# Block-wise linear attention ahead of two MLP layers: states kept without zero halves and met by the queries in quarters of the array, outputs and state sums in the score banks

## The chip, the cores and the metric

One core of a Trainium2 chip runs the whole kernel. The metric is the device time of one execution in microseconds (us); lower is better. The engines are PE (TensorE matmul; PEld is its loading of the stationary operand), DVE (VectorE), ACT (ScalarE), POOL (GpSimd) and SP, which issues the transfers. Each engine runs its own queue strictly in order; an instruction that must wait holds everything behind it on its engine.

## The reference

Attention with a decay per head, then two MLP layers. The part that matters:

```python
for b in range(nb):                        # blocks of a sequence, one after the other
    intra = einsum('bhic,bhjc->bhij', qb, kb) * Dmask      # Dmask[i,j] = lam**(i-j), i >= j
    intra = einsum('bhij,bhjd->bhid', intra, vb)
    inter = einsum('bhid,bhde->bhie', qb * lam_pow, kv_state)
    out[:, :, sl] = intra + inter
    kv_state = lam_block * kv_state + einsum('bhsd,bhse->bhde', kb * rev_pow, vb)
x = out with heads side by side            # (1536, 512)
h = x @ w_in;  x = where(h > 0, h, exp(min(h, 0)) - 1) @ w_out            # layer 0
h = x @ w_in2; y = (max(h, 0) + alpha * min(h, 0)) @ w_out2               # layer 1
```

There are 2 sequences of 768 positions, 8 heads of 64 channels, a model width of 512 and a hidden width of 2048. The kernel takes blocks of 128 positions (the decay makes that the same sum), so it has 12 blocks, 6 for each sequence. Block 0 and block 6 start from an empty state.

## The kernel before

**Attention, one block n.** The 8 heads stand as 4 pairs `pr`, head = 2*pr + `hs`. `load(n)` brings keys and queries (channels on the partitions, the two heads of a pair on partitions 0 to 63 and 64 to 127) and values and keys (positions on the partitions), 512 KB each. `scores(n)` makes the transposed scores in two PSUM banks, one for each `hs`, four pairs side by side (L201). `mask(n)` multiplies each bank by the decay and leaves the result in SBUF as `sm` (DVE, L208, two instructions). `scale(n)` makes the decayed keys `kd_t` and the decayed queries `qs_t` on POOL. `state(n)` sums keys times values into a bank of its own, `stp` (L223). `outputs(n)` makes, in a third kind of bank `po`, values times masked scores (L256, eight matmuls with 64 output rows each) and adds state times queries (L262): here the state of a pair is a 128 x 128 tile whose two off-diagonal quarters are zero, so one full-array matmul serves two heads. Blocks 0 and 6 have no L262. `new_state(n)` scales the old state on ACT (L235, four instructions) and adds `stp` on DVE (L241); the last block of a sequence has none. `keep(n)` copies the outputs into the MLP's operand as a rounded part `xh` (ACT, L274) and the rest `xl` (DVE, L275).

**MLP.** 96 items i: for each layer, four groups of four hidden tiles, three token chunks of 512 and the four tiles of a group. `up(i)` is 12 matmuls of 128 x 512 (three products of rounded parts and rests, four channel groups each, L362); ACT, DVE and POOL turn the result into `gh_t` and `gl_t`. `down(i)` is 12 matmuls (L400) and comes two items later (LAG = 2). Chunk 0 of x is blocks 0 to 3, so `up(0)` needs those four.

**Weights.** They arrive as 64-bit numbers; `split_w` makes a rounded part and a rest in six steps: ACT L125, DVE L126, L128 and L131, ACT L134, POOL L135. Each step is put off by a number of ticks of the program's own count and goes into its engine's queue where that tick falls. `wi` (into the hidden width) and `wo` (out of it) come in pairs of hidden tiles, 1 MB each.

**Order.** It is written out by hand (manual schedule). Four blocks come first (AHEAD), then one block with each item 0 to 7, then items alone:

```python
n = AHEAD + i
p_ = block_a(n)        # state(n); scores(n + 1); mask(n + 1)
up(i)
weights(i)
block_b(n, p_)         # outputs(n); new_state(n); keep(n); load(n + 4); scale(n + 2)
for e in range(4):
    if i < LAG: tick()
    else:       down(i - LAG, e)
```

So scores and mask of a block stand one `up` ahead of the outputs that use them. Items 0 and 1 have no `down`.

Of the kernel before, what the change touches and what calls it, by code (L numbers as in the profile page):

```python
# [7 lines left out]
F32 = mybir.dt.float32  # L8
# [3 lines left out]
ALU = mybir.AluOpType  # L12

B, H, S, D = 2, 8, 768, 64
C = 128
NBLK = B * S // C
PB = S // C
# [16 lines left out]
def attention_two_layers(  # L34
# [30 lines left out]
    def bank(name):  # L65
        return ps.tile([128, 512], F32, tag="ps", name=name)
# [30 lines left out]
    def load_w(c):  # L97
        n, part = divmod(c, 2)
        l, k = divmod(n, NPAIR)
        wi, wo = wts[l]  # L100
        r = wraw.tile([128, 2048], U32, tag="raw", name="raw")
        if part == 0:
            nc.sync.dma_start(
                out=r.rearrange("p (c f) -> p c f", c=NCC),
                in_=wi[:, k * 512:(k + 1) * 512].rearrange("(c p) f -> p c f", p=128))
        else:
            nc.sync.dma_start(
                out=r.rearrange("p (f e) -> p f e", f=2),
                in_=wo[k * 256:(k + 1) * 256, :].rearrange("(f p) e -> p f e", p=128))
        raw[c] = r  # L110
# [30 lines left out]
    def new_x(t, nm):  # L141
# [9 lines left out]
    rev = dm.rearrange("p s a i -> p a s i")[:, :, :, C - 1:C]  # L151
    sms = [wsp.tile([128, 1024], F32, tag=tag, name="sm").rearrange(
        "p (s a i) -> p s a i", s=2, a=NP) for tag in ("wil", "woh")]
    st2 = wsp.tile([128, 1024], F32, tag="wol", name="st").rearrange(
        "p (s a i) -> p s a i", s=2, a=NP)
    st = [st2[:, 0], st2[:, 1]]

    ld = {}
# [47 lines left out]
    def mask(n):  # L206
        for hs, p_ in enumerate(sc.pop(n)):
            nc.vector.tensor_tensor(  # L208
                out=sms[n % 2][:, hs], in0=p_.rearrange("p (a i) -> p a i", a=NP),
                in1=dm[:, hs], op=ALU.mult)  # L210

    cur = [0]

    def state(n):
        if n not in kd:
            return None
        kd_ = kd.pop(n)
        v_ = vs[n][0]
        p_ = bank("stp")
        for pr in range(NP):  # L220
            for hs in range(2):
                h = 2 * pr + hs
                nc.tensor.matmul(  # L223
                    out=p_[hs * 64:(hs + 1) * 64, pr * D:(pr + 1) * D], lhsT=kd_[:, h, :],
                    rhs=v_[:, h, :], start=pr == 0, stop=True, skip_group_check=True)
        return p_[:, 0:NP * D].rearrange("p (a d) -> p a d", a=NP)

    def new_state(n, p_):
        if p_ is None:
            return  # L230
        first = n % PB == 0
        old, new = st[cur[0]], st[1 - cur[0]]
        if not first:
            for pr in range(NP):
                nc.scalar.mul(new[:, pr, :], old[:, pr, :], lamc[:, pr, :])  # L235
        for hs in range(2):
            a, b = hs * 64, (hs + 1) * 64
            if first:
                nc.vector.tensor_copy(new[a:b, :, a:b], p_[a:b])
            else:  # L240
                nc.vector.tensor_tensor(  # L241
                    out=new[a:b, :, a:b], in0=p_[a:b], in1=new[a:b, :, a:b],
                    op=ALU.add)
        cur[0] = 1 - cur[0]

    def outputs(n):
        v_, _ = vs.pop(n)
        po = bank("po")
        sm_ = sms[n % 2]
        s_ = st[cur[0]]  # L250

        inter = n % PB > 0
        for pr in range(NP):
            for hs in range(2):
                h = 2 * pr + hs
                nc.tensor.matmul(  # L256
                    out=po[hs * 64:(hs + 1) * 64, pr * C:(pr + 1) * C],
                    lhsT=v_[:, h, :], rhs=sm_[:, hs, pr, :], start=pr == 0,
                    stop=not inter, skip_group_check=True)
        if inter:  # L260
            for pr in range(NP):
                nc.tensor.matmul(  # L262
                    out=po[:, pr * C:(pr + 1) * C], lhsT=s_[:, pr, :], rhs=qs[n][:, pr, :],
                    start=False, stop=True, skip_group_check=True)
        qs.pop(n, None)
        return po

    def keep(n, po):
        t, o = divmod(n * C, CH)
        if o == 0:  # L270
            new_x(t, "x")
        pv = po.rearrange("p (a i) -> p a i", a=NP)
        xh_ = xh[t][:, :, o:o + C]
        nc.scalar.copy(xh_, pv)  # L274
        nc.vector.tensor_tensor(  # L275
            out=xl[t][:, :, o:o + C], in0=pv, in1=xh_.bitcast(F32), op=ALU.subtract)
# [6 lines left out]
    def block_a(n):  # L283
        p_ = state(n)
        if n + 1 < NBLK:
            scores(n + 1)
            mask(n + 1)
        return p_

    def block_b(n, p_):  # L290
        po = outputs(n)
        new_state(n, p_)
        keep(n, po)
        if n + 4 < NBLK:
            load(n + 4)
        if n + 2 < NBLK:
            scale(n + 2)

    def begin():
        nc.sync.dma_start(out=row[:, 128:128 + H], in_=lam.rearrange("h a -> a h"))  # L300
        load(0)
        load(1)
        load_w(0)
        load(2)
        load(3)
# [32 lines left out]
        for s_ in st:  # L338
            nc.gpsimd.memset(s_, 0.0)
        scores(0)  # L340
        scale(0)
        mask(0)
        scale(1)
        split_w(0, (5, 6, 7, 9, 11), 4)

# [108 lines left out]

    with tc.manual_schedule():
        begin()
        for n in range(AHEAD):
            weights(n - AHEAD)
            p_ = block_a(n)
            for _ in range(3):  # L460
                tick()
            block_b(n, p_)
            if n < 2:
                load_w(2 - n)
            if n == 3:
                load_w(3)
            for _ in range(3):
                tick()
        for i, _ in enumerate(items):
            if i == 2:  # L470
                nc.sync.dma_start(out=alpha_sb, in_=alpha)
            if i == 20:
                nc.vector.tensor_scalar(
                    out=beta, in0=alpha_sb, scalar1=-1.0, scalar2=1.0, op0=ALU.mult,
                    op1=ALU.add)
            n = AHEAD + i
            p_ = block_a(n) if n < NBLK else None
            up(i)
            weights(i)
            if n < NBLK:  # L480
                block_b(n, p_)
            for e in range(4):
                if i < LAG:
                    tick()
                else:
                    for c0, c1 in parts(i - LAG, e):
                        down(i - LAG, e, c0, c1)
        for i in range(len(items) - LAG, len(items)):
            for e in range(4):
                for c0, c1 in parts(i, e):  # L490
                    down(i, e, c0, c1)
# [50 lines left out]
```

## Time and profile before

| | us |
|---|---|
| three timed runs | 586.23, 587.03, 587.05 (median 587.03) |
| the profiled execution, its own time | 586.05 |
| its span, first to last instruction | 584.1 |
| PE busy in the span | 575.3 (98%) |
| DVE, ACT, POOL busy | 271.8, 240.9, 227.9 |

The profile is of one execution. Positions below are us from the start of its span. 1.95 us of its time lie around the span.

### The profile page before, as it was taken

The numbers are of one execution on the slowest core, as the hardware profiler recorded it, in microseconds if no ns is written. First come the engines' busy times: TensorE is split into PE (matmuls) and PEld (weight loads), VectorE is DVE, ScalarE is ACT, GpSimd is POOL, SyncE is SP. The second block draws the span as 40 slices with busy tenths as digits, with TensorE's granted clock in tenths as the row PEclk, the third lists the DMA queues.
The fourth block names the chain that finished last, engine by engine and source line by source line (L and its number), as shares of the span: only waits on it lengthen the run. The fifth ranks groups of instructions, "written<-read, shape, count | busy, mean of one in ns | idle before, by whom it ended". The sixth has DMA issues, their size and how long they took to land.

```text
span 584.1 us, 7319 instructions
## 1 busy us (share of the span) xinstructions
PE 575.3 (98%) x2960; PEld 475.6 (81%) x2960; DVE 271.8 (47%) x363; ACT 240.9 (41%) x374; POOL 227.9 (39%) x156
## 2 busy tenths in 40 slices
PE   7999999999999999999999999999999999999997
PEld 6886788888888888888888888888888888888886
DVE  7777444753534542543645731443553551641332
ACT  2536354565435444544654442533324323432220
POOL 3756512454324344344233444434415334432221
PEclk9999999999999999999999999999999999999999
DMA  8985300342202122122102212222204110000111
GB/s 323 412 329 172 101 1 6 140 143 73 73 0 85 60 73 72 73 72 73 53 20 81 68 69 73 72 74 72 73 0 141 31 46 0 2 0 1 72 73 72
DMA packets 18307, 49.23 MB, mean 84 GB/s; under 512 B 1250, under 2 KB 1506, under 8 KB 18274
## 3 DMA queue, kind: packets, MB, share of 16 engines
q1 hardware_dynamic: 18274, 48.77, 23.7%
q8 instruction: 23, 0.38, 0.3%
q14 instruction: 10, 0.08, 0.0%
HBM read 45.62 MB, written 3.15 MB: 83 GB/s over the span
## 4 chain that ended last, share of the span: by engine, by line
PE 93%; DVE 2%; DMA 2%; ACT 1%; POOL 0%; issue 0%; SPq 0%; DVEq 0%
PE dn L400 44%; PE up L362 43%; DMA raw<-in_w1i 2%; PE sc L201 1%; PE po L256 1%; PE po L262 1%; PE warm L281 1%; DVE wt L128 1%; PE stp L223 1%; ACT st L235 0%; DVE acc L416 0%; DVE wt L131 0%; POOL wol L135 0%; DVE st L241 0%; DVE wt L126 0%
## 5 line engine op out<-in xcount | busy, mean ns | idle before, releaser
L384 POOL TENSOR_TENSOR gl_t<-g_t,gh_t 128x512 fp32r<-128x512 f32 x96 | 125.1, 1304 | 320.4 <-ACT gh_t L383 265.9
L373 ACT ACTIVATE r_t<-up 128x512 f32<-128x512 f32 x96 | 57.3, 597 | 187.2 <-PE up L362 187.2
L383 ACT CAST gh_t<-g_t 128x512 fp32r<-128x512 f32 x96 | 59.6, 621 | 110.9 <-DVE g_t L377 57.9
L416 DVE TENSOR_TENSOR acc<-dn,acc 128x512 f32<-128x512 f32 (+1 forms) x73 | 46.9, 676 | 75.7 <-PE dn L400 75.7
L400 PE MATMUL dn<-gh_t,wol 128*128 128x512 f32 x192 | 74.9, 390 | 1.3 <-POOL wol L135 1.3
L381 DVE SCALAR_TENSOR_TENSOR g_t<-r_t,beta,up 128x512 f32<-128x512 f32 x48 | 35.7, 743 | 86.2 <-ACT r_t L373 77.5
L400 PE MATMUL dn<-woh,gl_t 128*128 128x512 f32 (+1 forms) x196 | 75.4, 385 | 0.0
L400 PE MATMUL dn<-woh,gh_t 128*128 128x512 f32 (+1 forms) x196 | 75.4, 385 | 0.0
L400 PE MATMUL dn<-wol,gh_t 128*128 128x512 f32 (+1 forms) x196 | 75.4, 385 | 0.0
L400 PE MATMUL dn<-gh_t,woh 128*128 128x512 f32 x192 | 75.3, 392 | 0.0
L400 PE MATMUL dn<-gl_t,woh 128*128 128x512 f32 x192 | 74.8, 389 | 0.0
L377 DVE SCALAR_TENSOR_TENSOR g_t<-r_t,up 128x512 f32<-128x512 f32 x48 | 32.8, 683 | 63.0 <-ACT r_t L376 63.0
L362 PE MATMUL up<-xh,wih 128*128 128x512 f32 x192 | 52.2, 394 | 0.0
L362 PE MATMUL up<-xl,wih 128*128 128x512 f32 x192 | 51.4, 389 | 0.0
L362 PE MATMUL up<-xh,wil 128*128 128x512 f32 x192 | 51.4, 389 | 0.0
L362 PE MATMUL up<-yh,wih 128*128 128x512 f32 x192 | 51.3, 389 | 0.0
L362 PE MATMUL up<-yl,wih 128*128 128x512 f32 x192 | 51.3, 389 | 0.0
L362 PE MATMUL up<-yh,wil 128*128 128x512 f32 x192 | 51.3, 389 | 0.0
L126 DVE TENSOR_SCALAR wt<-wt 128x1024 uint32<-128x1024 uint32 x32 | 29.7, 927 | 33.5 <-ACT wt L125 33.5
L400 PEld LDWEIGHTS dn<-gh_t,wol 128*128 128x128 f32 x192 | 36.0, 188 | 9.2 <-POOL wol L135 1.7
L400 PEld LDWEIGHTS dn<-woh,gl_t 128*128 128x128 f32 x196 | 36.8, 188 | 7.4
L400 PEld LDWEIGHTS dn<-wol,gh_t 128*128 128x128 f32 x196 | 36.8, 188 | 7.4
(57 smaller groups left out, 796.2 us busy)
## 6 DMA issues: line engine op xcount, KB each, us to landing
raw<-in_w1i SPq DMA_DIRECT2D x8, 1024.0 KB, 5.6
raw<-in_w1o SPq DMA_DIRECT2D x8, 1024.0 KB, 4.8
raw<-in_w2i SPq DMA_DIRECT2D x8, 1024.0 KB, 5.4
raw<-in_w2o SPq DMA_DIRECT2D x8, 1024.0 KB, 4.9
blk<-in_kqT SPq DMA_DIRECT2D x12, 512.0 KB, 6.9
blk<-in_vk SPq DMA_DIRECT2D x10, 512.0 KB, 8.2
out<-acc SPq DMA_DIRECT2D x11, 256.0 KB, 2.1
blk<-in_vk SPq DMA_DIRECT2D x2, 256.0 KB, 6.4
```

The source lines that it names most:

```text
L126: later(gaps[0], lambda: nc.vector.tensor_scalar(out=tu, in0=tu, scalar1=3, scalar2=None, op0=ALU.logical_shift_left))
L128: later(gaps[1], lambda: nc.vector.scalar_tensor_tensor(out=tu, in0=lower, scalar=29, in1=tu, op0=ALU.logical_shift_right, op1=ALU.bitwise ...
L201: nc.tensor.matmul(out=ps_[hs][:, pr * C:(pr + 1) * C], lhsT=z[a:b, 0, pr, :], rhs=z[a:b, 1, pr, :], start=True, stop=True)
L223: nc.tensor.matmul(out=p_[hs * 64:(hs + 1) * 64, pr * D:(pr + 1) * D], lhsT=kd_[:, h, :], rhs=v_[:, h, :], start=pr == 0, stop=True, skip_ ...
L362: nc.tensor.matmul(out=p_, lhsT=w[:, cc, fo:fo + 128], rhs=x[t][:, cc, :], start=n == 0, stop=n == 3 * NCC - 1)
L373: nc.scalar.activation(r, p_, AF.Relu, scale=-1.0)
L377: later(1, lambda: nc.vector.scalar_tensor_tensor(out=g, in0=r, scalar=-1.0, in1=p_, op0=ALU.add, op1=ALU.max))
L381: later(1, lambda: nc.vector.scalar_tensor_tensor(out=g, in0=r, scalar=beta[:, f:f + 1], in1=p_, op0=ALU.mult, op1=ALU.add))
L383: later(2, lambda: nc.scalar.copy(gh_, g))
L384: later(3, lambda: nc.gpsimd.tensor_tensor(out=gl_, in0=g, in1=gh_.bitcast(F32), op=ALU.subtract))
L400: nc.tensor.matmul(out=p_, lhsT=a, rhs=b, start=first and n == 0, stop=last and n == 2)
L416: nc.vector.tensor_tensor(out=a, in0=p_, in1=a, op=ALU.add)
```

## The change

States are kept as 64 x 64 blocks, one for each head: a pair's two heads lie on partitions 0 to 63 and 64 to 127 of the same 64 columns. State times queries becomes eight matmuls for each block, 64 rows by 64 columns of the array each, in the order (o, hs) = (0,0), (1,0), (0,1), (1,1), where `o` is the half of the output partitions (pair pr = 2*pp + o). Outputs are written into the two banks in which the block's scores were, state sums into the other half of the first of them; the banks `po` and `stp` go. The new state is made by four DVE instructions (scale and add in one), behind the last state-times-queries matmul into the first bank; the four ACT instructions of before go. `keep` works on each bank by itself: two ACT and two DVE instructions of 256 columns in place of one each of 512, and ACT's first one comes behind DVE's reading of the state sums in the same bank. Since x's channels now stand in another order on the partitions, layer 0's `wi` is loaded by four transfers of 64 partitions in place of one of 128. The block's work is written in another order.

```diff
-        if part == 0:
+        if part == 0 and l == 0:
+            for o in range(2):
+                for hs in range(2):
+                    nc.sync.dma_start(
+                        out=r.rearrange("p (s a f) -> p s a f", s=2, a=2)[
+                            o * 64:(o + 1) * 64, hs],
+                        in_=wi[:, k * 512:(k + 1) * 512].rearrange(
+                            "(a o s d) f -> o s d a f", a=2, o=2, s=2)[o, hs])
+        elif part == 0:
...
+    def outputs(n):
...
+        for pp in range(2):
+            for o, hs in QUAD:
+                pr = 2 * pp + o
                 nc.tensor.matmul(
+                    out=p_[hs][o * 64:(o + 1) * 64, pp * C:(pp + 1) * C],
+                    lhsT=v_[:, 2 * pr + hs, :], rhs=sm_[:, hs, pr, :], start=pp == 0,
+                    stop=n % PB == 0, skip_group_check=True)
+        kd_ = kd.pop(n, None)
+        if kd_ is not None:
+            for pr in range(NP):
+                for hs in range(2):
...
+                        out=p_[0][hs * 64:(hs + 1) * 64, c0:c0 + D], lhsT=kd_[:, h, :],
+                        rhs=v_[:, h, :], start=False, stop=True, skip_group_check=True)
+        if n % PB:
...
+                    nc.tensor.matmul(
+                        out=p_[hs][o * 64:(o + 1) * 64, pp * C:(pp + 1) * C],
+                        lhsT=s_[a:b, pr, :], rhs=qs[n][a:b, pr, :], start=False, stop=True,
...
     def new_state(n, p_):
-        if not first:
             for pr in range(NP):
-                nc.scalar.mul(new[:, pr, :], old[:, pr, :], lamc[:, pr, :])
...
+                nc.vector.scalar_tensor_tensor(
+                    out=new[:, pr, :], in0=old[:, pr, :], scalar=lamc[:, pr, :],
+                    in1=p_[:, pr, :], op0=ALU.mult, op1=ALU.add)
...
+    def block(n):
+        p_, more = outputs(n)
+        if more:
+            new_state(n, p_)
+        keep(n, p_)
...
+    def ahead(n):
+        if n < NBLK:
+            scores(n)
+            mask(n)
...
-        scores(0)
+        ahead(0)
         scale(0)
-        mask(0)
+        ahead(1)
         scale(1)
...
         for n in range(AHEAD):
             weights(n - AHEAD)
-            p_ = block_a(n)
+            block(n)
             for _ in range(3):
                 tick()
-            block_b(n, p_)
+            if n + 2 <= AHEAD:
+                ahead(n + 2)
...
-            p_ = block_a(n) if n < NBLK else None
+            if n < NBLK:
+                block(n)
             up(i)
             weights(i)
             if n < NBLK:
-                block_b(n, p_)
+                ahead(n + 1)
```

PE's queue at items 0 and 1, before. `sc` are scores, `po<-sm,blk` outputs from the masked scores, `po<-qs_t,st` state times queries, `stp` state sums. The rows begin with the scores of block 5, then `up(0)`, the outputs of block 4, the scores of block 6, `up(1)` and the outputs of block 5.

```order
L201 MATMUL sc<-blk 128x128 x8
L362 MATMUL up<-xh_205,wih 128x512 x4
L362 MATMUL up<-xh_205,wil 128x512 x4
L362 MATMUL up<-xl_206,wih 128x512 x4
L256 MATMUL po<-sm,blk 64x128 x8
L262 MATMUL po<-qs_t,st 128x128 x4
L201 MATMUL sc<-blk 128x128 x8
L362 MATMUL up<-xh_205,wih 128x512 x4
L362 MATMUL up<-xl_206,wih 128x512 x4
L362 MATMUL up<-xh_205,wil 128x512 x4
L256 MATMUL po<-sm,blk 64x128 x8
L262 MATMUL po<-qs_t,st 128x128 x4
```

The same place after the change. Block 4's outputs are already done ahead of `up(0)`; L212 are scores, L239 outputs from the masked scores, L249 state sums, L259 state times queries.

```order
L371 MATMUL up<-xh_203,wih 128x512 x4
L371 MATMUL up<-xh_203,wil 128x512 x4
L371 MATMUL up<-xl_204,wih 128x512 x4
L212 MATMUL sc<-blk 128x128 x8
L239 MATMUL sc<-sm,blk 64x128 x8
L259 MATMUL sc<-qs_t,st 64x128 x8
L371 MATMUL up<-xh_203,wih 128x512 x4
L371 MATMUL up<-xl_204,wih 128x512 x4
L371 MATMUL up<-xh_203,wil 128x512 x4
L212 MATMUL sc<-blk 128x128 x8
L239 MATMUL sc<-sm,blk 64x128 x8
L249 MATMUL sc<-blk,kd_t 64x64 x8
```

The outputs of blocks 5 and 6 now follow their own scores directly; an `up` stood between them before.

DVE's queue at the same place, before: the mask of block 5, new state and `xl` of block 4, `g_t` of item 0, then the three steps of the first `wo` split with the mask of block 6 among them, then `xl` of block 5.

```order
L208 TENSOR_TENSOR sm<-sc,dm 128x512 x2
L241 TENSOR_TENSOR st<-stp,st 64x4x64 x2
L275 TENSOR_TENSOR xl_447<-po,xh_446 128x4x128
L377 SCALAR_TENSOR_TENSOR g_t<-r_t,up 128x512
L126 TENSOR_SCALAR wt<-wt 128x1024
L128 SCALAR_TENSOR_TENSOR wt<-raw,wt 128x1024
L208 TENSOR_TENSOR sm<-sc,dm 128x512 x2
L131 SCALAR_TENSOR_TENSOR wt<-raw,wt 128x1024
L275 TENSOR_TENSOR xl_447<-po,xh_446 128x4x128
```

After the change, from the second `wi` split to the mask of block 6:

```order
L136 TENSOR_SCALAR wt<-wt 128x1024
L138 SCALAR_TENSOR_TENSOR wt<-raw,wt 128x1024
L141 SCALAR_TENSOR_TENSOR wt<-raw,wt 128x1024
L273 SCALAR_TENSOR_TENSOR st<-st,qp,sc 128x64 x4
L286 TENSOR_TENSOR xl_418<-sc,xh_417 128x2x128 x2
L219 TENSOR_TENSOR sm<-sc,dm 128x512 x2
L386 SCALAR_TENSOR_TENSOR g_t<-r_t,up 128x512
L136 TENSOR_SCALAR wt<-wt 128x1024
L138 SCALAR_TENSOR_TENSOR wt<-raw,wt 128x1024
L286 TENSOR_TENSOR xl_418<-sc,xh_417 128x2x128 x2
L141 SCALAR_TENSOR_TENSOR wt<-raw,wt 128x1024
L219 TENSOR_TENSOR sm<-sc,dm 128x512 x2
```

The mask of block 5 now stands behind the split, the new state and `xl` of block 4, and the mask of block 6 behind all of the `wo` split and `xl` of block 5.

SP's queue at the start, before and after: the last transfer of block 1, the first `wi` and the transfers of block 2 and 3.

```order
L169 DMA blk<-in_vk 128x1024
L103 DMA raw<-in_w1i 128x4x512
L166 DMA blk<-in_kqT 128x1024
L169 DMA blk<-in_vk 128x1024
L166 DMA blk<-in_kqT 128x1024
```

```order
L180 DMA blk<-in_vk 128x1024
L107 DMA raw<-in_w1i 64x2x512 x4
L177 DMA blk<-in_kqT 128x1024
L180 DMA blk<-in_vk 128x1024
L177 DMA blk<-in_kqT 128x1024
```

Four transfers of 64 partitions stand ahead of block 2's keys and queries where one of 128 stood.

## Rows read from the trace of the kernel before

**Rows 1.** The profile's page: the span, and each engine's busy time.

```profile
span 584.1 us, 7319 instructions
PE 575.3 (98%) x2960; PEld 475.6 (81%) x2960; DVE 271.8 (47%) x363; ACT 240.9 (41%) x374; POOL 227.9 (39%) x156
```

**Rows 2.** The chain that ended last, 40 to 100 us: start, length, work.

```profile
59.87 0.62 PE stp L223 x16
60.49 1.09 PE sc L201 x16
61.58 2.97 PE up L362 x12
64.54 1.02 PE po L256 x16
65.57 1.09 PE po L262 x8
66.66 2.75 PE dn L400 x12
...
96.08 2.72 PE up L362 x12
```

**Rows 3.** Waits of PE, 10 to 75 us: total, times, longest.

```profile
PE sc L201 <- DMA blk<-in_kqT: 2.3, 1, 2.3
PE dn L400 <- POOL wol L135: 1.3, 1, 1.3
PE po L262 <- DVE st L241: 0.5, 1, 0.5
```

**Rows 4.** Timeline of PE, 10 to 23 us: start, length, instruction.

```profile
10.72 0.69 PE L223 MATMUL stp<-blk,kd_t 128*64 128x64 f32 x16
13.68 1.93 PE L201 MATMUL sc<-blk 64*128 64x128 f32 x16 [2.27 <-DMA blk<-in_kqT]
15.53 1.93 PE L256 MATMUL po<-sm,blk 128*64 128x128 f32 x16
```

**Rows 5.** Two stretches: length, busy us by engine, PEclk, DMA share, GB/s.

```profile
14.00:16.00 2.00, 2.00 (x20) 1.78 (x19) 1.67 (x3) 0.00 (x0) 1.06 (x1) 0.50 1.04 424
...
44.00:48.00 4.00, 2.72 (x23) 1.73 (x22) 1.49 (x3) 2.62 (x5) 2.36 (x1) 1.00 0.71 231
```

**Rows 6.** Timeline of DVE, 13 to 48 us.

```profile
28.06 0.68 DVE L126 TENSOR_SCALAR wt<-wt 128x1024 uint32<-128x1024 uint32 x1
28.78 1.22 DVE L128 SCALAR_TENSOR_TENSOR wt<-raw,wt 128x1024 uint32<-128x1024 uint32 x1
30.03 1.23 DVE L131 SCALAR_TENSOR_TENSOR wt<-raw,wt 128x1024 uint32<-128x1024 uint32 x1
...
39.47 1.96 DVE L128 SCALAR_TENSOR_TENSOR wt<-raw,wt 128x1024 uint32<-128x1024 uint32 x1
41.35 1.27 DVE L208 TENSOR_TENSOR sm<-sc,dm 128x512 f32<-128x512 f32 x2
```

**Rows 7.** Groups by line and shape, 0 to 75 us: busy, mean ns, idle before.

```profile
L275 DVE TENSOR_TENSOR xl<-po,xh 128x512 fp32r<-128x512 f32 x9 | 6.2, 692 | 3.3 <-ACT xh L274 3.1
...
L274 ACT CAST xh<-po 128x512 fp32r<-128x512 f32 x9 | 5.1, 571 | 9.0 <-PE po L256 8.7 <-PE po L262 0.3
L241 DVE TENSOR_TENSOR st<-stp,st 64x256 f32<-64x256 f32 x12 | 5.1, 422 | 9.4 <-ACT st L235 9.2
```

**Rows 8.** Timeline of ACT, 33 to 47 us.

```profile
36.91 0.62 ACT L383 CAST gh_t<-g_t 128x512 fp32r<-128x512 f32 x1 [1.77 <-DVE g_t L377]
37.44 1.17 ACT L125 ACTIVATE wt<-raw 128x1024 f32<-128x1024 f32 x1
43.80 1.05 ACT L134 CAST woh<-wt 128x1024 fp32r<-128x1024 f32 x1 [5.19 <-DVE wt L131]
44.75 0.59 ACT L373 ACTIVATE r_t<-up 128x512 f32<-128x512 f32 x1
```

**Rows 9.** Transfers: issues by line, KB each, us from issue to landing.

```profile
raw<-in_w1i SPq DMA_DIRECT2D x8, 1024.0 KB, 5.6
```

**Rows 10.** Timeline of PE, 28 to 48 us: the first `down`.

```profile
45.32 0.50 PE L400 MATMUL dn<-gh_t,woh 128*128 128x512 f32 x1
```

More of the change, by code (lines that the diff above doesn't have):

```diff
@@ L153, in attention_two_layers @@
         "p (s a i) -> p s a i", s=2, a=NP) for tag in ("wil", "woh")]
-    st2 = wsp.tile([128, 1024], F32, tag="wol", name="st").rearrange(
-        "p (s a i) -> p s a i", s=2, a=NP)
+    st2 = wsp.tile([128, 1024], F32, tag="wol", name="st")[:, 0:2 * NP * D].rearrange(
+        "p (s a d) -> p s a d", s=2, a=NP)
     st = [st2[:, 0], st2[:, 1]]
@@ L206, in mask @@
     def mask(n):
-        for hs, p_ in enumerate(sc.pop(n)):
+        for hs, p_ in enumerate(sc[n]):
             nc.vector.tensor_tensor(
@@ L212, in attention_two_layers @@
     cur = [0]
[L214 to L222, printed above, removed]
-                nc.tensor.matmul(
-                    out=p_[hs * 64:(hs + 1) * 64, pr * D:(pr + 1) * D], lhsT=kd_[:, h, :],
-                    rhs=v_[:, h, :], start=pr == 0, stop=True, skip_group_check=True)
-        return p_[:, 0:NP * D].rearrange("p (a d) -> p a d", a=NP)
+    QUAD = [(o, hs) for hs in range(2) for o in range(2)]
@@ new lines, in outputs @@
+    def outputs(n):
+        v_ = vs.pop(n)[0]
+        p_ = sc.pop(n)
+        sm_ = sms[n % 2]
+        for pp in range(2):
+            for o, hs in QUAD:
+                pr = 2 * pp + o
+                nc.tensor.matmul(
+                    out=p_[hs][o * 64:(o + 1) * 64, pp * C:(pp + 1) * C],
[5 more added lines that the diff above has]
+                for hs in range(2):
+                    h = 2 * pr + hs
+                    c0 = 2 * C + pr * D
+                    nc.tensor.matmul(
+                        out=p_[0][hs * 64:(hs + 1) * 64, c0:c0 + D], lhsT=kd_[:, h, :],
+                        rhs=v_[:, h, :], start=False, stop=True, skip_group_check=True)
+        if n % PB:
+            s_ = st[cur[0]]
+            for pp in range(2):
+                for o, hs in QUAD:
+                    pr = 2 * pp + o
+                    a, b = hs * 64, (hs + 1) * 64
+                    nc.tensor.matmul(
+                        out=p_[hs][o * 64:(o + 1) * 64, pp * C:(pp + 1) * C],
+                        lhsT=s_[a:b, pr, :], rhs=qs[n][a:b, pr, :], start=False, stop=True,
+                        skip_group_check=True)
+            qs.pop(n)
+        return p_, kd_ is not None
@@ L228, in new_state @@
     def new_state(n, p_):
-        if p_ is None:
-            return
-        first = n % PB == 0
+        p_ = p_[0][:, 2 * C:2 * C + NP * D].rearrange("p (a d) -> p a d", a=NP)
         old, new = st[cur[0]], st[1 - cur[0]]
-        if not first:
+        if n % PB == 0:
+            nc.vector.tensor_copy(new, p_)
+        else:
             for pr in range(NP):
-                nc.scalar.mul(new[:, pr, :], old[:, pr, :], lamc[:, pr, :])
[L236 to L243, printed above, removed]
@@ L244, in new_state @@
-        cur[0] = 1 - cur[0]
[L246 to L266, printed above, removed]
@@ L268, in keep @@
-    def keep(n, po):
+                nc.vector.scalar_tensor_tensor(
+                    out=new[:, pr, :], in0=old[:, pr, :], scalar=lamc[:, pr, :],
+                    in1=p_[:, pr, :], op0=ALU.mult, op1=ALU.add)
+        cur[0] = 1 - cur[0]
+    def keep(n, p_):
         t, o = divmod(n * C, CH)
@@ L271, in keep @@
             new_x(t, "x")
[L272 to L276, printed above, removed]
+        for hs in range(2):
+            pv = p_[hs][:, 0:2 * C].rearrange("p (a i) -> p a i", a=2)
+            xh_ = xh[t][:, 2 * hs:2 * hs + 2, o:o + C]
+            nc.scalar.copy(xh_, pv)
+            nc.vector.tensor_tensor(
+                out=xl[t][:, 2 * hs:2 * hs + 2, o:o + C], in0=pv, in1=xh_.bitcast(F32),
+                op=ALU.subtract)
     def run_up(n):
@@ L281, in run_up @@
             nc.tensor.matmul(out=pw[:, 0:C], lhsT=warm, rhs=warm, start=True, stop=True)
[L283 to L293, printed above, removed]
+    def block(n):
[3 more added lines that the diff above has]
+        keep(n, p_)
         if n + 4 < NBLK:
@@ L337, in begin @@
                 data1=warm, initial=1.0, op0=ALU.mult, op1=ALU.add)
-        for s_ in st:
-            nc.gpsimd.memset(s_, 0.0)
-        scores(0)
+        ahead(0)
         scale(0)
-        mask(0)
+        ahead(1)
         scale(1)
```

## The prediction

> **What bounds the kernel now.** I read the page first: PE is busy 575.3 of 584.1 us, every other engine less than half [rows 1]. So PE's own list is the time, plus the few places where PE stands still. The chain that ended last says the same in the stretch with a block in each item: PE follows PE, state sums 0.62, scores 1.09, `up` 2.97, outputs 1.02, state times queries 1.09, `down` 2.75, in sum 9.54 for an item with a block, where an `up` alone takes 2.72 [rows 2]. The reader is to see that the L262 part is 1.09 of these 9.54. Then I asked what PE waits for between 10 and 75 us: 2.3 for block 2's keys and queries, 1.3 for the first `wol`, 0.5 for a new state [rows 3]. Between 13.68, where block 2's scores start behind that first wait [rows 4], and 45.32, the first `down` [rows 10], lie 31.64 us, 0.5 of them waiting, so 31.1 of work; the 1.3 for `wol` follows inside that `down`.
>
> **PE's own work.** State times queries goes from four full-array matmuls in 8 records, 1.09, to eight of 64 by 64 in quarters. No row shows quarters. If all four quarters worked at once it would be two rounds in place of four, 0.5 of 1.09; if only two did, it would cost what the outputs do, eight matmuls with 64 rows out, 1.02 [rows 2]. The nearest row are the state sums, also eight matmuls in 16 records that write 64 by 64 blocks: 0.62. I take 0.61, a gain of 0.48 a block. Ten blocks have it: 1 to 5 and 7 to 11, so 2.4 for each five. The state sums of block 1 ran at 10.72, inside the wait for block 2's keys [rows 4]; now they stand behind that block's scores and cost their 0.6. Outputs, scores and the other state sums cost the same in their new banks. PE's list from 13.68 to the first `down` thus loses 2.4 and gains 0.6: 31.1 becomes 29.3.
>
> **DVE's chain.** The masks now stand on PE's path: outputs of block n need the mask that DVE takes up only behind the new state and `xl` of the block before, and behind whatever step of a split falls there. What a block costs DVE, by the slope between 692 ns at 512 columns and 422 at 256 (1.05 ns a column and 0.15 fixed) [rows 7]: four new-state instructions of 64 columns, 0.21 each, 0.85; two `xl` halves of 0.42. In between DVE waits for ACT's first `xh` half, which now comes behind the new state: 571 ns at 512 columns [rows 7] makes 0.36 for a half, and I add 0.12 for handing over, a choice: 0.48. A mask pair is 1.27, a half of it 0.64; the split steps 0.68, 1.22 and 1.23 [rows 6]. So a block costs 0.85 + 0.48 + 0.84 + 1.27 = 3.4 and a split 3.1. Before, `xl` of a block was all that stood between one mask and the next apart from the split, and PE had an `up` of slack from items 0 on.
>
> Walked from block 2's scores, which end at 15.55 (start 13.68, length as in [rows 4]), with ends of DVE: mask 2 16.9; L126 and L128 of the first `wi` split 18.8; state 1 19.65, hand-over and `xl` 20.97; L131 22.2; mask 3 23.5; state 2, hand-over, `xl` 25.65; mask 4 26.9; block 3 29.1; the second split 32.9 (its ACT step, 1.17 [rows 8], is done by 29.75); block 4 35.05; mask 5, its halves 35.7 and 36.3. Then item 0: ACT casts `wih` (as the 1.05 cast) and makes r, 0.59, and an exponential as long, DVE makes g by 37.55, ACT `gh_t`, 0.62, and L125, 1.17 [rows 8], to 39.45; DVE's L126 and L128 (1.96, as beside POOL at 39.47 [rows 6]) to 42.2; `xl` of block 5 43.1; L131 44.3; mask 6 44.95 and 45.6.
>
> PE along it (an output pass can begin on the first half of a mask and ends 0.8 behind the second): block 3's outputs wait 0.2 and end 24.3; block 4's wait 1.15, end 27.7. With state sums and state times queries to 28.9, `up(0)` to 31.9, scores of block 5 to 33.0. Block 5's outputs wait 2.7 and 0.35 more for the second half, to 37.1; state times queries 37.7; `up(1)` 40.7; scores of block 6 41.8; its outputs wait 3.15 and 0.35, to 46.35; state sums, `up(2)`, scores of block 7: the first `down` at 51.0. The waits are 0.2 + 1.15 + 3.05 + 3.5 = 7.9. Before it stood at 45.32, and 1.28 of `wol` wait followed, so 46.6: now `wol` is long there, and the 0.5 for the new state goes too, as that state is made ahead of PE's next block. Check: 7.9 − (2.4 − 0.6) − 1.8 = 4.3, against 51.0 − 46.6 = 4.4. From item 3 on a `down` stands between scores and outputs, 2.75 that cover the mask and one block of DVE; I cost it at nothing, and PE keeps the 2.4 of blocks 7 to 11. Net: 4.4 − 2.4 = +2.0. The four ACT multiplications of a block that go are costed at nothing: DVE stood idle for them, 9.2 over all blocks [rows 7], but of PE's waits only the 0.5 on the new state hung on it [rows 3], and that is counted.
>
> **Clock.** After the wait of 2.27 the granted clock was 0.50 from 14 to 16 us; after the 1.28 for `wol` it stayed 1.00 [rows 5]. At 0.50 scores and outputs took 3.72 where 2.11 is usual [rows 2, 4], 1.6 lost. The two waits of 3 and 3.5 lie nearer the first, so I let the clock fall after both: behind block 5 the next wait takes the loss up, behind block 6 nothing does, +1.6. Bounds 0 and 1.6.
>
> **Loads.** The first `wi` stands ahead of block 2's keys and queries, for which PE waits already, so a delay there is paid in full. It was one transfer of 1024 KB, 5.6 us from issue to landing [rows 9]; now four of 64 partitions with the same bytes and the same pieces. Bounds: nothing, or, if 64 partitions take only half the rate of 424 GB/s [rows 5], 5.0 us in place of 2.5 for 1.05 MB: +2.5. No row decides it; I take the middle, 1.2. The other seven `wi` loads are ahead of need.
>
> The Trainium skill (SBUF — State Buffer, section "Door 1: The DMA port swizzle") says that partitions 0 to 63 reach only half of the ports a transfer can use, with 196 GB/s measured where 128 partitions gave 328, and its section on two DMAs that two such transfers hardly overlap; by the page the sum would have 2.5 here in place of 1.2. The trace before has no such transfer and neither supports nor contradicts it.
>
> **Sum.** 586.05 + 2.0 + 1.6 + 1.2 = 590.85 for an execution like the profiled one. The median of the three runs stands 0.98 above that one, so 591.8.
>
> **Rivals.** First, the forecast with the loads at half rate: 1.3 more, 593.1. For it speaks that each half of the partitions comes in a transfer of its own; against, that the other half can run beside it, since a queue of SP issues them at once. The Trainium skill's rule on ports, named above, would make it so.
>
> Second, the same waits, but the clock holds and the loads cost nothing: 588.05 + 0.98 = 589.0. For it: only one wait of 2.27 has shown a fall, and four transfers carry the same bytes.
>
> Third, on the other side: DVE keeps ahead of PE. If `xl` and the split steps come earlier than I walk them (the ACT step done sooner, hand-overs shorter, steps of a split falling behind the mask), the outputs of blocks 5 and 6 wait only for their bare mask, 0.64 and some 0.4, 1.05 each, 2.1 in all; the clock holds. Then 2.1 − 1.8 − 1.8 − 2.4 = −3.9: 583.1. It decides from where PE's waits from 13.68 to the first `down` come to less than 1.8 + 1.8 + 2.4 = 6.0, against my 7.9. For it: DVE is busy 47% [rows 1]. Against: its work in this stretch is three splits and the chain above, with no gap but the hand-overs.
>
> Fourth, quarters run two at a time, 1.02: up to the first `down` DVE sets the place and nothing changes, later 0.07 a block is left of 0.48, +2.05: 593.9. For it, the outputs in [rows 2]; against, the state sums.
>
> **How the numbers follow.** Forecast 0.35, with 590.3 to 593.3 its own range (half of the clock or the loads' terms away); half-rate loads 0.22; waits alone 0.22; DVE ahead 0.13; quarters in pairs 0.08. The range leaves out the part of the third rival below 587.0, and what lies above 595.5 (half-rate loads and pairs together): 587.0 to 595.5. What a measurement can tell from no change is about 0.2%, 1.2 us, so 585.9 to 588.2: faster 0.15 (third rival and a little of the second), same 0.10 (the second's lower half), slower 0.75.
>
> **What would show it.** PE's waits on DVE's `sm` ahead of the outputs of blocks 5 and 6, near 3 us each and some 8 with those of blocks 3 and 4; the wait on `wol` gone; the first `down` near 51, up to 54 with clock and loads; the granted clock low just behind block 6's mask; the wait for block 2's keys at 3.5 in place of 2.3, and a smaller GB/s in the first 16 us; L259 in some 0.6 and an item with a block at 9.06 in place of 9.54. Wrong it would be made above all by waits under 6 in that stretch: an error of 0.5 in each of the four new states, hand-overs and `xl` pairs would be enough. Wrong upward: a mask late behind a `down` in items 3 to 7 too, where I cost it at nothing.

## The result, and the profile after

The changed kernel takes 589.79 us (median of 5 runs, 589.27 to 591.17) where the kernel before took 587.03 (5 runs, 585.93 to 587.79): a ratio of 1.0054, with a 95% interval of 1.0036 to 1.0072. It is slower by some 3 us. The profiled execution took 589.27 and its span is 587.5, against 584.1.

The first lines of the page, as in [rows 1]:

```profile
span 587.5 us, 7537 instructions
PE 572.8 (98%) x3040; PEld 472.7 (80%) x3040; DVE 271.2 (46%) x389; ACT 232.8 (40%) x354; POOL 225.9 (38%) x154
```

PE is busy 2.5 us less than before and the span is 3.4 longer. What PE waits for in the whole run (total, times, longest), as in [rows 3]; a wait of 1.1 at the very start, which the kernel before has too, is left out:

```profile
PE sc L212 <- DMA blk<-in_kqT: 5.0, 2, 4.5
PE sc L239 <- DVE sm L219: 4.9, 6, 2.3
```

The waits of before for `wol` and for a state are gone; the one for block 2's keys has doubled (2.27 to 4.48; the other 0.5 is for block 1's), and six for masks are new. Where they lie, on the timeline of PE between 15 and 53 us:

```profile
15.60 2.08 PE L212 MATMUL sc<-blk 64*128 64x128 f32 x16 [4.48 <-DMA blk<-in_kqT]
17.61 1.97 PE L239 MATMUL sc<-sm,blk 128*64 128x128 f32 x16
19.36 1.07 PE L249 MATMUL sc<-blk,kd_t 128*64 128x64 f32 x16
20.36 1.08 PE L259 MATMUL sc<-qs_t,st 64*64 64x128 f32 x16
...
37.60 0.44 PE L239 MATMUL sc<-sm,blk 128*64 128x128 f32 x4 [2.34 <-DVE sm L219]
38.20 1.46 PE L239 MATMUL sc<-sm,blk 128*64 128x128 f32 x12 [0.16 <-DVE sm L219]
39.59 1.13 PE L259 MATMUL sc<-qs_t,st 64*64 64x128 f32 x16
40.65 1.69 PE L371 MATMUL up<-xh,wih 128*128 128x512 f32 x4
...
46.69 0.44 PE L239 MATMUL sc<-sm,blk 128*64 128x128 f32 x4 [1.45 <-DVE sm L219]
47.29 0.88 PE L239 MATMUL sc<-sm,blk 128*64 128x128 f32 x12 [0.16 <-DVE sm L219]
...
52.61 0.50 PE L409 MATMUL dn<-gh_t,woh 128*128 128x512 f32 x1
```

Read from the bottom: the first `down` begins at 52.61. Before, it stood at 45.32 and waited 1.28 [rows 3, 10], so 46.60: the kernel has lost 6.0 us up to there. Of these 1.9 are there already when block 2's scores begin, at 15.60 in place of 13.68 [rows 4]. From there to the end of the span it takes 534.9 us where before took 537.5: 2.6 won back. 6.0 − 2.6 is the 3.4 of the spans.

Where they are won shows in the chain that ended last, one item with a block (start, length, work), as in [rows 2]:

```profile
55.63 1.02 PE sc L239 x16
56.66 0.46 PE sc L249 x16
57.12 0.60 PE sc L259 x16
57.72 2.96 PE up L371 x12
60.68 1.09 PE sc L212 x16
61.77 2.95 PE dn L409 x12
64.72 1.02 PE sc L239 x16
```

State times queries is 0.60 in place of 1.09, and an item 9.09 in place of 9.54. Two neighbours move as well in this reading, the state sums (0.46 in place of 0.62) and the `down` (2.95 in place of 2.75); together they cancel but for 0.04.

### The profile page after: what moved, and what is told of

Same layout as the page of the kernel before. It is cut to its first block, busy times and chain, and to the rows that moved or that the text cites. A ratio compares the mean times of both kernels' runs of the same rounds, so it can differ in the third digit from the quotient of the medians.

```text
span 587.5 us, 7537 instructions
## 1 busy us (share of the span) xinstructions
PE 572.8 (98%) x3040; PEld 472.7 (80%) x3040; DVE 271.2 (46%) x389; ACT 232.8 (40%) x354; POOL 225.9 (38%) x154
## 4 chain that ended last, share of the span: by engine, by line
PE 92%; DVE 3%; DMA 2%; ACT 1%; SPq 1%; POOL 0%; issue 0%; DVEq 0%; ACTq 0%
PE dn L409 44%; PE up L371 44%; DMA blk<-in_kqT 2%; PE sc L239 1%; PE sc L212 1%; PE sc L259 1%; DVE wt L141 1%; DVE sm L219 1%; DVE wt L138 1%; DVE st L273 1%; PE sc L249 1%; SPq L107 1%; DVE acc L425 0%; POOL wil L145 0%; ACT wt L135 0%; DVE xl L286 0%
## 5 line engine op out<-in xcount | busy, mean ns | idle before, releaser
L409 PEld LDWEIGHTS dn<-woh,gh_t 128*128 128x128 f32 x196 | 36.8, 188 | 7.5
```

Source lines behind the costliest of these rows:

```text
L409: nc.tensor.matmul(out=p_, lhsT=a, rhs=b, start=first and n == 0, stop=last and n == 2)
```

## The experiments

The theory: two things cost time up to the first `down`, the loads of 64 partitions and DVE's chain, behind which the masks now stand. The rivals: the number of transfers in place of their width; the clock; DVE having too much to do wherever the masks stand. The kernel before was run beside each set; its medians were 586.4 to 586.9 there, and 585.8 beside the last one. Each verdict goes by the ratio, the time of the run over that of the kernel before run beside it, with a 95% interval in brackets.

**Full loads.** The heads are handed over in another order, queries, keys, values and decays alike, so that each chunk of x holds natural channels and one transfer of 128 partitions does for `wi`.

```diff
-        if part == 0 and l == 0:
-            for o in range(2):
-                for hs in range(2):
-                    nc.sync.dma_start(
...
-        elif part == 0:
+        if part == 0:
...
-            xh_ = xh[t][:, 2 * hs:2 * hs + 2, o:o + C]
+            xh_ = xh[t][:, hs:NCC:2, o:o + C]
...
-        a = a.reshape(B, H, PB, C, D)
+        a = a.reshape(B, H, PB, C, D)[:, PERM]
...
```

> The changed kernel with one edit: the first layer's wi loads are single transfers of 128 partitions again (the heads are handed over in the order 0 2 1 3 4 6 5 7, so that each chunk of x keeps its channels in natural order; queries, keys, values and decays follow). Theory (four 64-partition transfers delay block 2's keys by about 2 us, and everything behind hangs on DVE's chain, which starts there): the wait for block 2's keys goes from 4.5 back to about 2.3, the first down moves some 2 us earlier, 587.3 to 587.9 in place of 589.8. Rival (the delay is taken up by the mask waits that follow): the mask waits grow by what the load wait loses, 589.5.

588.22 us, ratio 1.0027 (1.0013 to 1.0041), against 1.0054 (1.0036 to 1.0072) for the change: about half the loss goes, though the two intervals overlap at their ends. What PE waits for:

```profile
PE sc L229 <- DVE sm L209: 8.3, 8, 3.1
PE sc L202 <- DMA blk<-in_kqT: 2.3, 2, 2.0
```

The keys come in time again and save 2.7 us of waiting (5.0 to 2.3), but the mask waits grow by 3.4 (4.9 to 8.3), as PE arrives sooner at masks that DVE has not made. Theory and rival were each half right. In the profiled executions the first `down` moves only from 52.61 to 52.30; the one profiled here, 588.96, is among the longer ones of its kernel (587.02 to 589.22). Two rows of PE's timeline:

```profile
36.10 0.44 PE L229 MATMUL sc<-sm,blk 128*64 128x128 f32 x4 [3.08 <-DVE sm L209]
...
45.21 2.14 PE L229 MATMUL sc<-sm,blk 128*64 128x128 f32 x16 [2.99 <-DVE sm L209]
```

The second is followed by the half clock (2.14 for outputs that take 1.09), the first is not.

**Quarter loads in the kernel before.**

```diff
-        if part == 0:
+        if part == 0 and l == 0:
+            for o in range(2):
+                for s in range(2):
+                    nc.sync.dma_start(
+                        out=r.rearrange("p (s a f) -> p s a f", s=2, a=2)[
+                            o * 64:(o + 1) * 64, s],
...
```

> The kernel before with one edit: the first layer's wi loads are four transfers of 64 partitions each, same bytes, same places. Theory: the wait for block 2's keys grows from 2.3 to 4.2 to 4.6 and the GB/s between 8 and 14 us fall from about 400 to about 240; 2 us or a little more slower, 588.8 to 589.5. Rival (the transfers are only late in the changed kernel because of its own order): 587.0 as before.

592.35 us, ratio 1.0117 (1.0089 to 1.0145): 7 us slower (5.9 between the medians), far more than expected. Stretches of 2 us (length, busy time of PE, PEld, DVE, ACT and POOL, granted clock, DMA share, GB/s):

```profile
8.00:10.00 2.00, 2.00 (x36) 1.62 (x32) 2.00 (x5) 0.00 (x0) 0.00 (x0) 1.00 1.04 211
10.00:12.00 2.00, 0.87 (x14) 0.62 (x10) 1.96 (x5) 0.58 (x1) 0.95 (x1) 1.00 1.04 213
12.00:14.00 2.00, 0.69 (x16) 0.55 (x16) 0.41 (x1) 0.00 (x0) 1.33 (x2) 1.00 1.13 208
```

The transfers keep the DMA engines as busy as ever (share 1.04) and move half. Block 2's scores begin at 17.38 in place of 13.68. The later loads are late too: the second `wi` is issued at 14.74 in place of 11.80, the first `wo` at 22.34 in place of 18.47. So PE also waits for `kd_t` (1.6), `xh` (0.7), the first `woh` (0.9) and the first `wol` (1.7), and behind that last wait most matmuls of the first `down` take 0.63 in place of 0.39.

**Four full transfers in the kernel before.**

```diff
+            for c_ in range(NCC if l == 0 else 0):
+                nc.sync.dma_start(
+                    out=r.rearrange("p (c f) -> p c f", c=NCC)[:, c_],
+                    in_=wi[c_ * 128:(c_ + 1) * 128, k * 512:(k + 1) * 512])
...
```

> The kernel before with the first layer's wi loads in four transfers of 256 KB that each have all 128 partitions. If the 64 partitions are what slows the loads: 587.0, GB/s near 400 from 8 us on. If four issues in place of one (their time on SP, and the places that they take among the transfers under way) are what delays block 2's keys: as with four transfers of 64 partitions, 588.8 to 589.5.

586.14 us, ratio 1.0001 (0.9990 to 1.0011). The same stretches:

```profile
8.00:10.00 2.00, 2.00 (x39) 1.81 (x39) 1.91 (x5) 0.00 (x0) 0.44 (x1) 1.00 1.02 387
10.00:12.00 2.00, 1.36 (x32) 1.17 (x28) 1.96 (x5) 0.58 (x1) 1.84 (x2) 1.00 1.05 418
12.00:14.00 2.00, 0.57 (x10) 0.60 (x12) 1.30 (x3) 1.12 (x1) 0.00 (x0) 1.00 1.02 420
```

So it is the width and not the number; that the four issues put block 2's keys later in SP's queue (4.95 in place of 3.52) costs nothing. The Trainium skill (SBUF — State Buffer, "Door 1: The DMA port swizzle") has it so: half of the partitions reach half of the ports, 196 in place of 328 GB/s. Here it is 208 to 213 against 387 to 420, and that the four transfers together get no more agrees with its section "Can I just issue two DMAs to hit both halves?", where one transfer at partition 0 and one at 64 gave 6% more than a single one.

**Quarters in pairs, in the kernel before.**

```diff
...
+                for hs in range(2):
+                    a, b = hs * 64, (hs + 1) * 64
+                    nc.tensor.matmul(
+                        out=po[a:b, pr * C:(pr + 1) * C], lhsT=s_[a:b, pr, a:b],
+                        rhs=qs[n][a:b, pr, :], start=False, stop=True,
...
```

> The kernel before with state times queries in eight matmuls of 64 by 64 that use the two diagonal quarters alone (the zero halves are not read; nothing else changes). If it is four quarters at once that makes 0.60 of 1.09: here two work at once, some 1.0 a block, 586.4 as before. If leaving out the zero halves is what helps: 0.6 a block, 582 to 584.

586.32 us, ratio 0.9996 (0.9987 to 1.0005). Two rows of PE:

```profile
25.29 1.09 PE L264 MATMUL po<-qs_t,st 64*64 64x128 f32 x16
26.31 0.69 PE L223 MATMUL stp<-blk,kd_t 128*64 128x64 f32 x16
```

26.31 − 25.29 is 1.02: eight 64 by 64 matmuls on the two diagonal quarters cost nearly what four full ones do (1.09). Leaving out the zero halves is thus not what helps; of the two orders that were run, only the one that goes round all four quarters takes 0.60.

**Masks of blocks 5 and 6 early.**

```diff
-            if n + 2 <= AHEAD:
-                ahead(n + 2)
+            ahead(n + 2)
...
             if n < NBLK:
                 block(n)
+            if i == 0:
+                ahead(n + 2)
             up(i)
             weights(i)
-            if n < NBLK:
+            if 2 <= i and n < NBLK:
                 ahead(n + 1)
```

> The changed kernel with scores and masks of blocks 5 and 6 one block earlier (block 5's behind the outputs of block 3, block 6's behind those of block 4), all else in place. Theory (the masks stand behind a split and a block of DVE's work, only their place is at fault): the waits before the outputs of blocks 5 and 6, 2.5 and 1.6, go, and with them the clock's second fall (1.6 lost); a wait of up to 1.3 for the first wol can return; 585.0 to 587.0. Rival (DVE has too much to do up to there wherever the masks stand): the waits come back on the state, on xl or on wol, 588.5 or more.

589.57 us (587.76 to 593.26), ratio 1.0059 (1.0037 to 1.0082): nothing won, against the theory's 585.0 to 587.0. The waits of PE (the profiled execution is one of the shortest, 587.8):

```profile
PE sc L212 <- DMA blk<-in_kqT: 9.7, 4, 4.3
PE dn L409 <- POOL wol L145: 1.9, 2, 1.6
...
PE sc L239 <- DVE sm L219: 0.7, 3, 0.4
```

The mask waits are all but gone, and the keys of blocks 5 and 6, wanted earlier, are late by 3.1 and 1.0 behind the slow loads.

**Both.** Full loads and early masks.

> Loads of all 128 partitions and the masks of blocks 5 and 6 one block earlier, together. With the masks early alone, the waits on masks fell to 0.7 but those on keys grew to 9.7, as the slow loads hold up the keys of blocks 5 and 6; with full loads alone the mask waits are 8.3. Theory (two faults, each hiding the other): here the mask waits stay under 1.5, the waits for keys fall to 3 to 5, 583.5 to 585.5 where the kernel before has 586.4. Rival (DVE or the loads take what the masks give whatever the place): 587.5 or more.

586.73 us, ratio 1.0002 (0.9991 to 1.0012): the whole loss is undone. The theory's 583.5 to 585.5, a gain over the kernel before, did not come, nor did the rival's 587.5. Each edit is worth something beside the other: the early masks take 1.0027 (1.0013 to 1.0041) down to 1.0002, the full loads 1.0059 (1.0037 to 1.0082), and neither interval meets that of both together. What PE waits for:

```profile
PE sc L202 <- DMA blk<-in_kqT: 3.5, 2, 2.2
PE dn L399 <- ACT woh L134: 2.5, 1, 2.5
PE sc L229 <- DVE sm L209: 1.8, 3, 1.5
PE dn L399 <- POOL wol L135: 1.7, 1, 1.7
```

The wait has moved on to the weights of the first `down`, 4.2 us of it, and the clock stands at 0.50 from 48 to 52 us:

```profile
48.00:52.00 4.00, 4.00 (x10) 3.12 (x10) 2.54 (x5) 2.79 (x7) 3.91 (x4) 0.50 0.93 368
```

The span, 584.6, is 0.5 above that of the kernel before, and the two timelines of PE show where. The first `wol` matmul begins at 47.98 in place of 47.33, 0.65 later. The rest of that `down` takes 4.56 (to 52.54) in place of 2.50 (to 49.83), 2.06 lost at the low clock. From there to the `up` of item 8 it takes 43.91 (to 96.45) in place of 46.09 (to 95.92), 2.18 won. So the quarters do give their part in the items with a `down`, and the clock's fall takes it.

**Both, block 5 loaded ahead of the second `wi`.**

```diff
-            if n < 2:
-                load_w(2 - n)
+            if n == 1:
+                load_w(2)
+                load_w(1)
```

> As the kernel with both edits, and the load of the second wi pair behind that of block 5 in SP's queue in place of ahead of it. If what is left of waits for keys there is queueing behind that 1 MB: 2 us less waiting than with both edits alone, 582 to 584. If the places of the blocks in SBUF or the waits of the second wi split decide: no change or slower.

586.37 us, ratio 0.9992 (0.9981 to 1.0003): no difference that can be measured. The waits for keys are 3.4 in place of 3.5. The run could not have helped: in the kernel with both edits the two waits are for block 1's keys (1.29, until 8.08) and block 2's (2.19, until 13.30), and the second `wi` is issued at 12.09, behind both blocks.

**Full loads, the two waits filled.** Ten matmuls into an unread bank ahead of the outputs of blocks 5 and 6.

```diff
+        if n in (AHEAD + 1, AHEAD + 2):
+            run_up(10)
```

> The kernel with full loads, and ten matmuls into an unread bank ahead of the outputs of blocks 5 and 6 each, so that PE works through most of the two waits of 3 us. If the clock's fall behind block 6's wait (outputs, state sums and the start of up at half clock, 1.6 lost) is part of the time: the outputs of block 6 take 0.9 in place of 2.1, 586.4 to 587.0 in place of 588.2. If that loss is taken up by a later wait, or the clock falls anyway: 588.2.

587.83 us, ratio 1.0019 (1.0010 to 1.0028) against 1.0027 (1.0013 to 1.0041) without: 0.4 us, and the intervals overlap. In the two profiled executions the half clock behind block 6's mask is gone and the first `down` begins at 50.96 in place of 52.30, 1.34 less. Of that 0.15 is there ahead of block 6's outputs (45.21 and 45.06), so a fall costs about 1.2; how often it falls without the filling these runs do not settle. Most of the loss is not the clock: with the filling it is 1.00 in every stretch of 4 us from 8 to 52, and the span of 585.8 is still 1.7 above that of the kernel before.

**LAG 3.** One line (`LAG = 3`) in three kernels: with both edits, in the kernel before, and with full loads alone. It also gives `gh_t` and `gl_t` one buffer more.

> The kernel with both edits (full loads, masks of blocks 5 and 6 early) and each down three items behind its up in place of two (LAG 3), so that item 2, too, has no down and the first wo pair is wanted about one item later. With both edits alone the mask waits became waits of the first down: 2.5 for woh and 1.7 for wol, and 4 us at half clock behind them. Theory (DVE's work up to the first wo split is what binds, and PE's quarters only shorten a list that waits for it): these waits and the clock's fall go and the 4.8 of the quarters show, 580 to 583.5. Rival (the wait goes on to the next thing DVE makes, block 7's mask or the second wo split): 585.5 or more.

> The kernel before with LAG 3, as the measure for the run beside it. It waits 1.3 for the first wol and has no fall of the clock there: 585.0 to 586.6 in place of 586.7. If it gains as much as the changed kernel does, LAG and not the quarters is what the run beside it shows.

> Full loads and LAG 3, the masks of blocks 5 and 6 where the change has them. Theory: the waits of 3 us ahead of the outputs of blocks 5 and 6 stay, as they come ahead of any down, and nothing is won: 587.3 to 588.8 (588.2 without LAG 3). Rival (a place for the first down is all that was missing): 584 or less.

588.90 us, ratio 1.0040 (1.0026 to 1.0054); 588.96, ratio 1.0036 (1.0022 to 1.0049); 589.24, ratio 1.0046 (1.0031 to 1.0060). In that order; all three are slower than the kernel before. The theory missed on the first: the 4.2 of waiting for weights did not go but became one wait, for block 7's mask, as the rival said.

```profile
49.56 2.14 PE L229 MATMUL sc<-sm,blk 128*64 128x128 f32 x16 [6.67 <-DVE sm L209]
```

Yet DVE has little to do just there; its timeline in the same kernel, behind one row of ACT's timeline:

```profile
44.28 1.04 ACT L134 CAST woh<-wt 128x1024 fp32r<-128x1024 f32 x1 [4.57 <-DVE wt L131]
```

```profile
42.62 1.63 DVE L131 SCALAR_TENSOR_TENSOR wt<-raw,wt 128x1024 uint32<-128x1024 uint32 x1
46.51 0.69 DVE L376 SCALAR_TENSOR_TENSOR g_t<-r_t,up 128x512 f32<-128x512 f32 x1 [2.27 <-ACT r_t L375]
47.12 0.42 DVE L260 COPY st<-sc 128x256 f32<-128x256 f32 x1
48.16 0.76 DVE L276 TENSOR_TENSOR xl<-sc,xh 128x256 fp32r<-128x256 f32 x2 [0.62 <-ACT xh L275]
48.83 1.28 DVE L209 TENSOR_TENSOR sm<-sc,dm 128x512 f32<-128x512 f32 x2
```

The mask stands behind g of an item, g behind ACT's r, and ACT's r behind the cast of `woh` that waits for DVE's L131: a round trip between two engines, each in order. LAG 3 harms the kernel before too, where 585.0 to 586.6 was expected, with new waits for `xl` (1.6) and `kd_t` (1.1); so it shows nothing of what the quarters could give. With full loads alone it won nothing, as the theory said, though 589.24 lies above its 588.8.

**Both, the first `wo` split sooner.** The split stands ahead of `up(0)`.

```diff
-    when = {-1: [2], 0: [1], 2: [3]}
+    when = {-1: [2], 2: [3]}
...
             if i == 0:
                 ahead(n + 2)
+                split_w(1, (3, 4, 6, 9, 10), 0)
+                later(13, lambda: load_w(4))
```

> The kernel with both edits (LAG 2), and the first wo split ahead of up(0): its ACT step behind the xh of block 4, its DVE steps behind the mask of block 6 in the gaps that DVE had round g of item 0, woh ahead of item 1's r. With both edits alone the first down waited 2.5 for woh and 1.7 for wol, and 4 us at half clock followed; DVE then stood idle 2.2 in two places for ACT just ahead of that split. Theory (what is left is the chain of DVE and ACT steps up to the first wol, DVE's order and not its amount): woh is done near 42, the wait for it goes, that for wol falls to 0.5 to 1.5, and the clock's fall goes: 582.0 to 584.5 in place of 586.7, faster than the kernel before. Rival (the wait goes to block 7's mask or to the second wi, as it did to block 7's mask with LAG 3): 586 or more.

586.77 us, ratio 1.0011 (1.0002 to 1.0020): the theory's gain did not come. The wait for `woh` went from 2.5 to 0.3, and the one for `wol` from 1.7 to 3.9, and the rest of the first `down` again runs partly at the low clock (0.61 from 48 to 52 us). POOL says why `wol` is late:

```profile
37.32 2.49 POOL L135 TENSOR_TENSOR wil<-wt,wih 128x1024 fp32r<-128x1024 f32 x1 [6.62 <-ACT wih L134]
42.23 1.54 POOL L383 TENSOR_TENSOR gl_t<-g_t,gh_t 128x512 fp32r<-128x512 f32 x1 [2.41 <-ACT gh_t L382]
43.73 1.05 POOL L183 TENSOR_TENSOR kd_t<-blk,dm 128x512 f32<-128x512 f32 x1
44.75 1.26 POOL L190 TENSOR_TENSOR qs_t<-blk,qp 128x512 f32<-128x512 f32 x1
45.98 2.35 POOL L135 TENSOR_TENSOR wol<-wt,woh 128x1024 fp32r<-128x1024 f32 x1
```

`woh` is there at 43.7; POOL takes `wol` up at 45.98, behind `gl_t`, `kd_t` and `qs_t`. And the L128 of this split took 3.28 (37.62 to 40.90) beside POOL's `wil`, where it takes 1.22 alone [rows 6].

## Why the prediction was right, and where its sum was off

**The direction and the two causes: right.** 591.8 was forecast with a range of 587.0 to 595.5, and 589.8 measured. Loads and mask places are what the loss hangs on: with both undone it is gone (1.0002). The size was less well foreseen. 589.8 lies below the forecast's own 590.3 to 593.3 and nearer the second rival, waits alone, at 589.0; that rival was right that the clock adds nothing, and wrong that the loads do not. The forecast came as near as it did partly by luck, as its term for the loads was too small where others were too large.

**PE's quarters: right.** 0.61 forecast, 0.60 measured; an item 9.06 forecast, 9.09 measured; 2.4 for blocks 7 to 11, 2.6 measured from the first `down` to the end. The rival with two at a time is out, and the diagonal quarters show what it would have cost: 1.02. That 0.61 came out so well is in part luck: it was taken from the state sums, which are not quarters and move 64 columns where these move 128.

**DVE's chain: right in place.** These are rows of DVE in the changed kernel:

```profile
34.85 0.85 DVE L273 SCALAR_TENSOR_TENSOR st<-st,qp,sc 128x64 f32<-128x64 f32 x4
36.19 0.76 DVE L286 TENSOR_TENSOR xl<-sc,xh 128x256 fp32r<-128x256 f32 x2 [0.49 <-ACT xh L285]
36.87 1.28 DVE L219 TENSOR_TENSOR sm<-sc,dm 128x512 f32<-128x512 f32 x2
...
45.96 1.27 DVE L219 TENSOR_TENSOR sm<-sc,dm 128x512 f32<-128x512 f32 x2
```

State 0.85, hand-over 0.49, `xl` 0.76, mask 1.28, against 0.85, 0.48, 0.84 and 1.27. The masks of blocks 5 and 6 end at 38.15 and 47.23; the walk has 36.3 and 45.6, and with the 1.9 by which block 2's scores came later 38.2 and 47.5. (The walk starts from 15.55 where [rows 4] give 13.68 + 1.93 = 15.61, and its 42.2 is some 0.2 more than the lengths that it names add up to; neither matters here.) The waits themselves were put at 7.9 and came to 4.9 in the change, since PE too was late. Behind the wait for keys it took 5.77 (15.60 to 21.37) for what took 3.18 at the next block (to 24.55), 2.6 lost at half clock where the forecast reckoned with the 1.6 of before; and the second fall, behind block 5's mask, shortened block 6's wait. With full loads they are 8.3. The prediction's own sign of being wrong, waits under 6 as the place from which the rival on the faster side decides, was thus met, and the kernel was slower all the same: the sign took short waits to mean an early DVE. DVE did not run ahead, as the ends of its masks show, so that rival is out.

**Loads: mis-sized, and not paid in full.** 1.2 was put in as a middle between nothing and 2.5; the start of block 2's scores moved by 1.9, and the half rate is what the transfers show. In the change itself the rates from 8 to 14 us are 168, 281 and 238 GB/s, where the kernel before has 398, 420 and 412. The sentence "a delay there is paid in full" failed: the edit that gives the keys back in time wins 1.6 (1.0054 to 1.0027), with mask waits growing from 4.9 to 8.3. In the kernel before, which has no mask waits to take a delay up, the same loads cost 7. "The other seven `wi` loads are ahead of need" held only as long as the masks were late: with the masks early, keys that stand behind the second of them were late as well (3.1 and 1.0), and with full loads they were not.

**Clock: the failed term.** "Behind block 6 nothing does, +1.6". In the change the clock fell behind block 5's wait of 2.34, as outputs of 1.46 and an `up` beginning with 1.69 show, and block 6's wait took that up; behind block 6's wait, only 1.45 long since PE was late, it did not fall. So this term was 0. The granted clock in two stretches of the changed kernel, the second of which has block 6's wait; from 48 to 52 it is 1.00 too:

```profile
40.00:44.00 4.00, 4.00 (x28) 2.88 (x20) 2.98 (x3) 1.48 (x3) 4.00 (x3) 0.78 1.04 425
44.00:48.00 4.00, 2.39 (x34) 1.88 (x35) 3.23 (x5) 1.90 (x3) 1.76 (x2) 1.00 0.56 201
```

With full loads, where the waits are near the forecast (3.2 and 3.0 for 3.05 and 3.5), it falls behind block 6's wait alone of these two (0.62 from 44 to 48 us).

In the sum: 1.6 too much for the clock, 0.7 too little for the loads; the net of waits and quarters +1.5 (6.0 − 1.9 − 2.6) for the +2.0 forecast; and the median of the changed kernel lies 0.5 above its profiled execution where 0.98 was added. Together about −1.9 of the difference of −2.0; the rest is the time round the span (1.8 in place of 1.95). The shares come by subtraction: what the longer half clock behind the wait for keys cost is in the net of waits and quarters.

**What was not foreseen:** that undoing both causes gives the kernel before and no more. PE's work is shorter in the runs with both edits too, by 4.8 us by the forecast's sum, but its waits take the place: 9.7 us with both edits, 9.9 with block 5 sooner, 11.2 with LAG 3 and 7.5 with the first `wo` split sooner, against 4.1 in the kernel before (the 1.1 at the very start left out). As the order is moved they fall on masks, on `woh`, on block 7's mask or on `wol`, and the low clock in the rest of the first `down` costs 1.6 to 2.1 more in the three with LAG 2. That the chain of steps through DVE, ACT and POOL which makes the first weights holds PE there fits all these places, but it is argued and not shown: no run shortened that chain. Nor was PE kept at work through these waits in a kernel with both edits, which would have parted the clock's share from the chain's. Whether some order lets the 4.8 through stays open.

## What to carry to other kernels

An edit that shortens the busiest engine pays where that engine runs without waiting, here the items with a `down` (9.54 to 9.09), and paid nothing here in a start-up stretch where it waits for others. A layout that packs two halves better on one side can cost on the other: look what each transfer's partitions become. And two causes of waiting in one stretch need not add: here one edit alone won about 1.6, the other nothing, and both together the whole 3. Undo them one by one and together before you price either.

## What was unexpected of the hardware

Four transfers of 64 partitions moved 208 to 213 GB/s at a DMA share of 1.04 to 1.13, where four of 128 moved 387 to 420 at 1.02 to 1.05: the share does not tell that the rate is halved. A DVE step on two operands in SBUF (128x1024, L128) took 1.22 alone, 1.96 when it began at 39.47 [rows 6] under a `kd_t` of POOL's that ran to 40.34, and 3.28 when it began under POOL's 2.49 in the last run. Begun ahead of POOL's instruction it kept its time: 1.23 from 19.80 in the changed kernel, with a `kd_t` from 20.58. The Trainium skill (SBUF — State Buffer, "Who interferes with whom") says that a DVE instruction with two SBUF inputs contends with POOL's reads; the durations of 1.22, 1.96 and 3.28 agree. And the granted clock fell behind waits of 2.34 and 2.99 us but not behind one of 3.08: the length of a wait alone did not decide it.
